# Two heads side by side in the TensorE array for the product of keys and values, with the last 64 tokens padded by zero rows

## The chip, the cores and the metric

The kernel runs on one core of a Trainium2 chip. The metric is the device time of one execution in microseconds (us), of which less is better. It is the median over several executions.

## The reference, cut to what matters

The program computes linear attention without a softmax, a norm of each head's output, and two feed-forward layers over all 8 x 576 = 4608 tokens. The part that the change touches is the first product, `kv`:

```python
# q, k, v: [batch 8, heads 8, tokens 576, 64] float32
kv  = np.einsum('bhsd,bhse->bhde', k, v)         # 64 x 64 for each head
out = np.einsum('bhsd,bhde->bhse', q, kv)
rms = np.sqrt(np.mean(out * out, axis=-1, keepdims=True) + 1e-06)
x   = out / rms * g_norm                          # then [4608, 512]
h = x @ w_in;  x = (h * sigmoid(1.702 * h)) @ w_out      # 512 -> 2048 -> 512
h = x @ w_in2; x = (s * relu(h) ** 2 + b) @ w_out2
```

## The kernel before, in words

The feed-forward layers take nearly all of TensorE's time. Each layer goes over nine blocks of 512 tokens, and each block over 16 chunks of d_ff. One such chunk of one block is a step. In a step `mm1` (lines 312 to 314) makes 12 passes of 512 columns for the first product of the layer, and `mm2` (lines 360 to 362 in the first layer, 364 to 366 in the second) makes 12 more for the second product, two steps later. Operands are split into a high and a low part, which is why there are three passes to each chunk.

Attention runs beside the steps, ahead of the block that needs it. For a batch `kv_pair(bb, p)` (lines 163 to 176) is called four times, once for two heads that lie next to each other. Its operands are tiles of 128 tokens x 128 columns, the 64 columns of one head and then the 64 of the other. So a product over the tokens gives 128 x 128 numbers, of which only the two 64 x 64 blocks on the diagonal are used. The 576 tokens are four chunks of 128 (line 169) and a rest of 64 (line 170), which reads a tile with 64 partitions. Such a product of float32 operands runs as two passes on TensorE, each with its own load of weights (LDWEIGHTS, PEld in the profile). A call is therefore ten passes, eight at line 169 and two at line 170.

`kv_out` (lines 178 to 185) copies the diagonal blocks of a batch from PSUM into `kvbd`, whose other blocks were set to zero by GpSimd at the start (line 491). `att_u` (lines 200 to 213) multiplies the queries of 128 tokens by `kvbd`. Where 128 tokens belong to two batches, 64 to each, it makes two products of 64 columns of weights, one into PSUM partitions 0 to 63 (line 212) and one into partitions 64 to 127 (line 213). There are four such token tiles (numbers 4, 13, 22 and 31).

The order of the work on each engine is the order of the program's text. The loop over steps in the last part of the function calls, in a step, `mm1`, then what the table `beside` holds under "pe" (here `kv_pair` and `att_u` are put by `kv_at` and `tile_at`), and then `mm2`. So in a step that has one, a `kv_pair` stands between line 314 and line 360. Batches 0 and 1 have their eight calls in the text ahead of the loop; batches 2 to 7 have theirs, 24 calls, in the loop. `load_rem` fetches the rests of the keys and values of a batch by SyncE's DMA queue (line 149), after the last `kv_pair` of the batch before has read the same buffer.

Of the kernel before, what the change touches and what calls it, by code (L numbers as in the profile page):

```python
# [8 lines left out]
F32 = mybir.dt.float32  # L9
# [6 lines left out]
P = 128  # L16
B, H, S, D = 8, 8, 576, 64
NT, DM, DFF = 4608, 512, 2048
NP = H // 2          # head pairs
KD = DM // P         # chunks of d_model  # L20
KF = DFF // P        # chunks of d_ff
BT = 512             # tokens of a block
NB = NT // BT
TT = BT // P         # token tiles of a block
#: While the first layer's weights become float32, two blocks share them: (block, from, to) in d_ff
#: chunks; what such a part leaves is added up when the second layer loads it.
CUTS = (0, 4, 8, 12, KF)
HEAD = [(j, lo, hi) for lo, hi in zip(CUTS, CUTS[1:]) for j in range(2)]
PARTS = HEAD + [(j, 0, KF) for j in range(2, 2 * NB)]
WARM = 8             # products that wake the tensor engine's clock  # L30
POOL = 8             # weights that GpSimd helps to split, while VectorE has the most to do
SM = 512             # tokens of a batch in whole chunks of 128
NC = SM // P
#: Of a float64's upper word, read as a float32: the exponent below float32's least, and where
#: float32 ends.
W_LEAST = 2.0 ** -15
# [4 lines left out]
def tile_attn_moe_moe2(  # L41
# [15 lines left out]
):  # L57
    """Float32 products in three passes of float32r: each operand is split exactly into
    H (12 significant bits, rounded) and L = x - H (the other 12)."""
    nc = tc.nc  # L60

    const = ctx.enter_context(tc.tile_pool(name="const", bufs=1))
# [3 lines left out]
    lp = ctx.enter_context(tc.tile_pool(name="lp", bufs=2))  # L66
# [10 lines left out]
    mhalf = const.tile([P, H], F32, name="mhalf")  # L77
    warm = const.tile([P, H], F32, name="warm")
    kvbd = [const.tile([P, NP, P], F32, name=f"kvbd{i}") for i in range(2)]

# [1 line left out]
    w_in, w_out = {}, {}  # L82
# [4 lines left out]
    def spare(name, shape):  # L87
        """A tile where weights come later."""
        return wp.tile(shape, F32, tag=name, name=f"s_{name}")
# [6 lines left out]
    def to_f32(which, ph, f):  # L96
        """float64 words to float32, rounded to nearest even: the exponent is rebased by bits,
        the 29 bits that go are rounded to one count of the last place that is added.
        A generator: other instructions go between its own."""
        raw = w_raw.pop((which, ph, f))  # L100
        lo, hi = raw[:, :, 0], raw[:, :, 1]
        w = lp.tile([P, DM], U32, tag="wf", name="wf", bufs=2)
        nc.scalar.activation(out=w.bitcast(F32), in_=hi.bitcast(F32), func=ACTF.Abs)
        nc.scalar.activation(out=lo, in_=lo, func=ACTF.Copy, scale=2.0 ** -29)
        yield
        # what float32 has no exponent for: 0 below it, the largest above it
        nc.vector.tensor_scalar(
            out=w.bitcast(F32), in0=w.bitcast(F32), scalar1=W_LEAST, scalar2=W_MOST, op0=ALU.max, op1=ALU.min
        )
        yield  # L110
        nc.vector.tensor_scalar(
            out=w, in0=w, scalar1=3, scalar2=0x3FFFFFF8, op0=ALU.logical_shift_left, op1=ALU.bitwise_and
        )
        yield
        nc.vector.scalar_tensor_tensor(
            out=w, in0=hi, scalar=0xC0000000, in1=w, op0=ALU.bitwise_and, op1=ALU.bitwise_or
        )
        yield
        nc.vector.tensor_tensor(out=w, in0=w, in1=lo, op=ALU.add)
        w_raw[which, ph, f] = w.bitcast(F32)  # L120
        yield
# [20 lines left out]

# [1 line left out]
    kt, vt, rem = {}, {}, {}  # L144

    def load_rem(bb):
        for nm, src in (("k", k_rest), ("v", v_rest)):
            t = lp.tile([P // 2, H * D], F32, tag=f"{nm}rem", name=f"{nm}rem", bufs=1)
            nc.sync.dma_start(out=t, in_=src[bb])
            rem[nm, bb] = t  # L150

# [11 lines left out]
    def kv_pair(bb, p):  # L163
        if bb not in kvps:
            kvps[bb] = ps_a.tile([P, NP, P], F32, tag="a", name="kvps")
        o = kvps[bb]
        kk, vv = kt.pop((bb, p)), vt.pop((bb, p))
        for c in range(NC):
            nc.tensor.matmul(o[:, p, :], kk[:, c, :], vv[:, c, :], start=(c == 0), stop=False)  # L169
        nc.tensor.matmul(  # L170
            o[:, p, :],
            rem["k", bb][:, p * P:(p + 1) * P],
            rem["v", bb][:, p * P:(p + 1) * P],
            start=False,
            stop=True,
        )

# [11 lines left out]
    def load_q(i, place=None):  # L189
        if place is None:  # L190
            q_t[i] = lp.tile([P, NP, P], F32, tag="q", name="qt", bufs=2)
        else:
            q_t[i] = spare(place, [P, NP, P])
        nc.sync.dma_start(out=q_t[i], in_=q[i].rearrange("p (a t) -> p a t", t=P))

    def early(i):
        # the first tiles use the PSUM of the feed-forward's sums, before there are any
        return dict(pool=ps_y, tag=f"y{i % TT}") if i < TT + 2 else dict(pool=ps_a, tag="a")

    def att_u(i):  # L200
        """Token-major q . kv of all heads."""
        qt = q_t.pop(i)
        e = early(i)
        u = u_t[i] = e["pool"].tile([P, H, D], F32, tag=e["tag"], name="u")
        b0, b1 = i * P // S, (i * P + P - 1) // S
        for p in range(NP):
            o = u[:, 2 * p:2 * p + 2, :]
            if b0 == b1:
                nc.tensor.matmul(o, qt[:, p, :], kvbd[b0 % 2][:, p, :], start=True, stop=True)  # L209
            else:  # L210
                m = b1 * S - i * P
                nc.tensor.matmul(o[0:m], qt[:, p, 0:m], kvbd[b0 % 2][:, p, :], start=True, stop=True)
                nc.tensor.matmul(o[m:P], qt[:, p, m:P], kvbd[b1 % 2][:, p, :], start=True, stop=True)
# [49 lines left out]

# [1 line left out]
    y_dram = {}  # L265
# [28 lines left out]

# [1 line left out]
    steps = [(j, f, lo, hi) for j, lo, hi in PARTS for f in range(lo, hi)]  # L296
    begin = {}                    # step at which a part begins
    for n, (j, f, lo, hi) in enumerate(steps):
# [84 lines left out]

# [1 line left out]
    beside = {}  # L385
# [8 lines left out]
    def tile_at(i, n, n_norm, n_turn, slot="turn"):  # L394
        """One tile of attention: what it is made of at step n, and when it is normed and turned."""
        at(n, "pe", att_u, i)
        at(n, "act", att_sq, i)
        at(n, "r", att_r, i)
        at(n_norm, "norm", att_norm, i)
        at(n_turn, slot, att_turn, i)  # L400
        early = "0" if slot == "pe" else ""
        at(n_turn, "xh" + early, att_xh, i)
        at(n_turn, "xl" + early, att_xl, i)

    def kv_at(bb, p, n):
        at(n, "pe", kv_pair, bb, p)
        if p + 2 < NP:
            at(n, "load", load_kv, bb, p + 2)
# [9 lines left out]

    # second block: most of it is begun before the steps
    at(5, "load", load_rem, 2)  # L420
# [9 lines left out]
    at(3, "xl0", att_xl, TT + 3)  # L430
    # third block
    n0 = begin[1, CUTS[-2]]
# [7 lines left out]
    tile_at(2 * TT + 3, n0 + 1, n0 + 2, n0 + 2)  # L440
    # the others
    for v_ in range(3, NB):
# [4 lines left out]
        for t in range(TT):  # L447
            n = n0 + 4 + 3 * t
# [9 lines left out]

    # weights: the first layer's in the order they are needed, then the second's through DRAM
    def need(w):  # L460
# [3 lines left out]

    order = sorted(((which, f) for f in range(KF) for which in (0, 1)), key=need)
    AHEAD = 3                     # before the first step
    convs = {}                    # by step
    first_w2 = 2 * KF + 2
    when = [(m - AHEAD, 0) + w for m, w in enumerate(order)]
# [12 lines left out]
    when = sorted([(n0 - 13 + f, 0, f) for f in range(KF)] + [(n0 - 5 + f, 1, f) for f in range(KF)])  # L482
# [5 lines left out]
    with tc.manual_schedule():  # L488
        make_identity(nc, ident)
        for t in kvbd:  # L490
            nc.gpsimd.memset(t, 0.0)
        nc.gpsimd.memset(mhalf, -0.5)
        # the activation table, and the tensor engine's clock, before there is work
        nc.scalar.activation(out=warm, in_=mhalf, func=ACTF.Sigmoid)
        o = ps_h.tile([P, BT], F32, tag="h", name="warm")
# [202 lines left out]
```

## Time and profile before

| | |
|---|---|
| median of three runs | 1697.47 us (1696.31 to 1697.64) |
| profiled execution: span, first to last instruction | 1694.9 us |
| of it, TensorE busy (PE) | 1677.7 us, 99% |
| weight loads busy (PEld) | 1391.6 us, 82% |
| VectorE / ScalarE / GpSimd busy | 716.4 / 574.6 / 72.4 us |
| passes on TensorE recorded | 7724 |

The profile is one execution. Its own time is known by its span only; the median of the runs is 2.6 us over that span, which takes in what lies ahead of the first instruction and behind the last. PE is the row of matmuls, PEld that of weight loads. A matmul's record lasts longer than the time until the next one starts, as matmuls are pipelined, so what a pass takes is read from the distance between starts.

### The profile page before, as it was taken

The page shows a single profiled execution, that of the slowest core. Times are in us where ns is not written, and L with a number is a line of the kernel's source. Part 1 is how long each engine was busy: PE and PEld are TensorE (multiplying, and loading weights), DVE is VectorE, ACT ScalarE, POOL GpSimd, SP SyncE. Part 2 cuts the span into 40 slices and gives each one's busy share as a digit, 9 for nine tenths or more (in the row PEclk, how much of TensorE's full clock was granted, in tenths as well). Part 3 has the DMA queues.
Part 4 walks back from the last instruction along what each step waited for, and adds up shares of the span by engine and source line. Part 5 has one row for each costly group of instructions (what it writes and reads, how often), then busy time and mean ns, then how long its engine had stood idle before and what let it go on. Part 6 is the DMA issues. An engine that isn't in the chain of part 4 may idle for free.

```text
span 1694.9 us, 19170 instructions
## 1 busy us (share of the span) xinstructions
PE 1677.7 (99%) x7724; PEld 1391.6 (82%) x7724; DVE 716.4 (42%) x1128; ACT 574.6 (34%) x957; POOL 72.4 (4%) x50
## 2 busy tenths in 40 slices
PE   8899999999999999999999999999999999999999
PEld 7688888888888888888888888888888888888887
DVE  5776634444353444444455533333233333333322
ACT  4566533333333333333334322222222222222222
POOL 3200100000000000001000000000000000000000
PEclk9999999999999999999999999999999999999999
DMA  6354523141313312121334210101010101000000
GB/s 224 118 174 153 178 95 92 56 123 58 131 53 103 94 57 91 59 75 57 112 107 144 92 50 1 50 1 50 1 50 1 50 1 38 12 20 31 1 25 25
DMA packets 57112, 120.78 MB, mean 71 GB/s; under 512 B 6848, under 2 KB 6848, under 8 KB 57024
## 3 DMA queue, kind: packets, MB, share of 16 engines
q1 hardware_dynamic: 57024, 119.57, 21.6%
q8 instruction: 60, 0.98, 0.3%
q14 instruction: 28, 0.23, 0.0%
HBM read 85.98 MB, written 33.55 MB: 71 GB/s over the span
## 4 chain that ended last, share of the span: by engine, by line
PE 97%; DVE 1%; DMA 1%; ACT 1%; issue 0%; SPq 0%; ACTq 0%; DVEq 0%
PE h L312 15%; PE h L313 15%; PE h L314 15%; PE acc L360 8%; PE acc L365 8%; PE acc L364 8%; PE acc L366 8%; PE acc L362 8%; PE acc L361 8%; PE kvps L169 2%; PE u L209 1%; PE xtp L238 1%; PE kvps L170 1%; DMA vt<-in_v 1%; DMA wraw<-in_w_out 0%
## 5 line engine op out<-in xcount | busy, mean ns | idle before, releaser
L312 PE MATMUL h<-xh,wih 128*128 128x512 f32 (+1 forms) x1156 | 452.0, 391 | 0.0
L314 PE MATMUL h<-xl,wih 128*128 128x512 f32 (+1 forms) x1156 | 449.1, 389 | 0.0
L313 PE MATMUL h<-xh,wil 128*128 128x512 f32 (+1 forms) x1156 | 449.1, 388 | 0.0
L314 PEld LDWEIGHTS h<-xl,wih 128*128 128x128 f32 x1156 | 217.0, 188 | 45.3
L312 PEld LDWEIGHTS h<-xh,wih 128*128 128x128 f32 x1156 | 217.2, 188 | 44.2
L313 PEld LDWEIGHTS h<-xh,wil 128*128 128x128 f32 x1156 | 217.1, 188 | 43.8
L325 DVE SCALAR_TENSOR_TENSOR g<-g,s_sb 128x512 f32<-128x512 f32 x144 | 108.3, 752 | 333.0 <-ACT g L324 333.0
L360 PE MATMUL acc<-gh,woh 128*128 128x512 f32 x576 | 230.9, 401 | 3.4 <-DVE xl L259 3.4
L324 ACT ACTIVATE g<-h 128x512 f32<-128x512 f32 x144 | 86.0, 597 | 430.4 <-PE h L314 430.4
L362 PE MATMUL acc<-gl,woh 128*128 128x512 f32 x576 | 225.6, 392 | 0.0
L361 PE MATMUL acc<-gh,wol 128*128 128x512 f32 x576 | 225.5, 391 | 0.1
L364 PE MATMUL acc<-woh,gh 128*128 128x512 f32 x576 | 224.1, 389 | 0.0
L365 PE MATMUL acc<-wol,gh 128*128 128x512 f32 x576 | 224.1, 389 | 0.0
L366 PE MATMUL acc<-woh,gl 128*128 128x512 f32 x576 | 224.1, 389 | 0.0
L321 ACT ACTIVATE g<-h 128x512 f32<-128x512 f32 x144 | 86.0, 597 | 348.7 <-PE h L314 348.6
L322 DVE TENSOR_TENSOR g<-g,h 128x512 f32<-128x512 f32 x144 | 98.9, 687 | 235.7 <-ACT g L321 235.4
L342 DVE SCALAR_TENSOR_TENSOR gl<-g,b_sb,gh 128x512 fp32r<-128x512 f32 x144 | 108.0, 750 | 175.4 <-PE acc L366 130.4
L334 ACT ACTIVATE gh<-g,b_sb 128x512 fp32r<-128x512 f32 x144 | 104.3, 724 | 118.7 <-DVE g L325 118.7
L340 DVE TENSOR_TENSOR gl<-g,gh 128x512 fp32r<-128x512 f32 x144 | 100.6, 699 | 96.7 <-PE acc L362 94.2
L360 PEld LDWEIGHTS acc<-gh,woh 128*128 128x128 f32 x576 | 108.7, 189 | 28.0 <-DVE xl L259 3.6
L362 PEld LDWEIGHTS acc<-gl,woh 128*128 128x128 f32 x576 | 108.7, 189 | 23.3
L332 ACT CAST gh<-g 128x512 fp32r<-128x512 f32 x144 | 89.5, 622 | 111.1 <-DVE g L322 111.1
(75 smaller groups left out, 1294.9 us busy)
## 6 DMA issues: line engine op xcount, KB each, us to landing
wraw<-in_w_in SPq DMA_DIRECT2D x32, 512.0 KB, 4.1
wraw<-in_w_out SPq DMA_DIRECT2D x32, 512.0 KB, 4.0
y<-ev SPq DMA_DIRECT2D x60, 256.0 KB, 2.2
yraw<-y SPq DMA_DIRECT2D x60, 256.0 KB, 3.9
out<-ev SPq DMA_DIRECT2D x36, 256.0 KB, 2.3
qt<-in_q SPq DMA_DIRECT2D x34, 256.0 KB, 4.5
w<-wf SPq DMA_DIRECT2D x32, 256.0 KB, 4.4
w2f<-w SPq DMA_DIRECT2D x32, 256.0 KB, 2.8
```

The costliest lines, as they stand in the source:

```text
L312: nc.tensor.matmul(o, wh[:, cs], xh[:, c, t0:t1], start=(c == 0), stop=False)
L313: nc.tensor.matmul(o, wl[:, cs], xh[:, c, t0:t1], start=False, stop=False)
L314: nc.tensor.matmul(o, wh[:, cs], xl[:, c, t0:t1], start=False, stop=(c == KD - 1))
L325: nc.vector.scalar_tensor_tensor(out=g, in0=g, scalar=s_sb[:, 0:1], in1=g, op0=ALU.mult, op1=ALU.mult)
L334: nc.scalar.activation(out=gh, in_=g_t[n], func=ACTF.Identity, bias=b_sb[:, 0:1])
L342: nc.vector.scalar_tensor_tensor(out=gl, in0=g, scalar=b_sb[:, 0:1], in1=gh, op0=ALU.add, op1=ALU.subtract)
L360: nc.tensor.matmul(o, wh[:, ds_], gh, start=first, stop=False)
L361: nc.tensor.matmul(o, wl[:, ds_], gh, start=False, stop=False)
L362: nc.tensor.matmul(o, wh[:, ds_], gl, start=False, stop=last)
L364: nc.tensor.matmul(o, gh[:, ds_], wh, start=first, stop=False)
L365: nc.tensor.matmul(o, gh[:, ds_], wl, start=False, stop=False)
L366: nc.tensor.matmul(o, gl[:, ds_], wh, start=False, stop=last)
```

## The change

`kv_pair` no longer multiplies two heads by two heads. For each chunk of tokens it makes two products of 64 columns of weights by 64 moving columns, one for each head. The first head's goes to PSUM partitions 0 to 63, the second's to partitions 64 to 127, and the two alternate. The rest of 64 tokens is read from tiles of 128 partitions, whose upper 64 partitions GpSimd sets to zero once at the start; the DMA goes on filling the lower 64. These tiles are allocated once and no longer taken from the pool `lp`, which held one buffer of each as well. Comments are taken out, which moves line numbers.

```diff
+    rem_t = {nm: const.tile([P, H * D], F32, name=f"{nm}rem") for nm in "kv"}
     kvbd = [const.tile([P, NP, P], F32, name=f"kvbd{i}") for i in range(2)]
...
     def load_rem(bb):
         for nm, src in (("k", k_rest), ("v", v_rest)):
-            t = lp.tile([P // 2, H * D], F32, tag=f"{nm}rem", name=f"{nm}rem", bufs=1)
-            nc.sync.dma_start(out=t, in_=src[bb])
-            rem[nm, bb] = t
+
+            nc.sync.dma_start(out=rem_t[nm][0:S - SM], in_=src[bb])
+            rem[nm, bb] = rem_t[nm]
...
         kk, vv = kt.pop((bb, p)), vt.pop((bb, p))
-        for c in range(NC):
-            nc.tensor.matmul(o[:, p, :], kk[:, c, :], vv[:, c, :], start=(c == 0), stop=False)
-        nc.tensor.matmul(
-            o[:, p, :],
-            rem["k", bb][:, p * P:(p + 1) * P],
-            rem["v", bb][:, p * P:(p + 1) * P],
-            start=False,
-            stop=True,
-        )
+
+        for c in range(NC + 1):
+            for h in range(2):
+                hs = slice(h * D, (h + 1) * D)
+                if c < NC:
+                    a, m = kk[:, c, hs], vv[:, c, hs]
+                else:
+                    w = slice(p * P + h * D, p * P + (h + 1) * D)
+                    a, m = rem["k", bb][:, w], rem["v", bb][:, w]
+                nc.tensor.matmul(o[hs, p, hs], a, m, start=(c == 0), stop=(c == NC))
...
         make_identity(nc, ident)
+        for t in rem_t.values():
+            nc.gpsimd.memset(t[S - SM:P], 0.0)
         for t in kvbd:
             nc.gpsimd.memset(t, 0.0)
         nc.gpsimd.memset(mhalf, -0.5)
```

TensorE's queue around the first `kv_pair` of batch 2 stood so before (output tile, operands, the output's partitions x columns, and how many products; each float32 product is two passes):

```order
L312 MATMUL h<-xh,wih_1115 128x512
L313 MATMUL h<-xh,wil_1116 128x512
L314 MATMUL h<-xl,wih_1115 128x512
L169 MATMUL kvps<-vt,kt 128x128 x4
L170 MATMUL kvps<-vrem,krem 128x128
L360 MATMUL acc_1341<-gh,woh_1405 128x512
L361 MATMUL acc_1341<-gh,wol_1406 128x512
```

And now, at a `kv_pair` of the same batch:

```order
L314 MATMUL h<-xh,wih_1202 128x512
L315 MATMUL h<-xh,wil_1203 128x512
L316 MATMUL h<-xl,wih_1202 128x512
L178 MATMUL kvps<-vt,kt 64x64 x8
L178 MATMUL kvps<-vrem,krem 64x64 x2
L362 MATMUL acc_1379<-gh,woh_1503 128x512
L363 MATMUL acc_1379<-gh,wol_1504 128x512
```

The place between the 12 passes of `mm1` and the 12 of `mm2` is the same; five products became ten of a quarter of the size.

GpSimd's queue at the start, before:

```order
masks.py:199 AFFINE_SELECT ident<-ident 128x128
L491 MEMSET kvbd_90 128x512
L491 MEMSET kvbd_91 128x512
L492 MEMSET mhalf 128x8
L227 TENSOR_TENSOR r<-ms,mhalf 128x8 x4
```

And now:

```order
masks.py:199 AFFINE_SELECT ident<-ident 128x128
L493 MEMSET krem 64x512
L493 MEMSET vrem 64x512
L495 MEMSET kvbd_92 128x512
L495 MEMSET kvbd_93 128x512
L496 MEMSET mhalf 128x8
L229 TENSOR_TENSOR r<-ms,mhalf 128x8 x4
```

Two memsets stand ahead of those of `kvbd` and `mhalf`. The queues of VectorE, ScalarE and SyncE (the DMAs) hold the same instructions in the same order as before.

## Rows read from the trace of the kernel before

**Rows 1.** The page, parts 1 and 2: busy time by engine, and TensorE's granted clock.

```profile
PE 1677.7 (99%) x7724; PEld 1391.6 (82%) x7724; DVE 716.4 (42%) x1128; ACT 574.6 (34%) x957; POOL 72.4 (4%) x50
...
PEclk9999999999999999999999999999999999999999
```

**Rows 2.** The page, part 4: the chain that ended last, by engine.

```profile
PE 97%; DVE 1%; DMA 1%; ACT 1%; issue 0%; SPq 0%; ACTq 0%; DVEq 0%
```

**Rows 3.** Windows: stretch, length, busy us (instructions) by engine, clock, DMA share, GB/s.

```profile
60.00:400.00 340.00, 339.94 (x1608) 282.05 (x1607) 185.33 (x319) 153.56 (x267) 23.34 (x13) 1.00 0.38 123
400.00:900.00 500.00, 500.00 (x2360) 415.24 (x2359) 227.05 (x374) 168.44 (x287) 29.35 (x17) 1.00 0.26 84
900.00:1694.00 794.00, 791.04 (x3490) 654.65 (x3489) 265.83 (x368) 224.99 (x356) 0.00 (x0) 1.00 0.10 33
```

**Rows 4.** Timeline of PE around one `kv_pair`: start us, length us, instructions merged.

```profile
639.74 0.39 PE L314 MATMUL h<-xl,wih 128*128 128x512 f32 x1
639.97 1.05 PE L169 MATMUL kvps<-vt,kt 128*128 128x128 f32 x8
640.95 0.48 PE L170 MATMUL kvps<-vrem,krem 64*128 64x128 f32 x2
641.37 0.50 PE L360 MATMUL acc<-gh,woh 128*128 128x512 f32 x1
641.70 0.40 PE L361 MATMUL acc<-gh,wol 128*128 128x512 f32 x1
```

**Rows 5.** Lines 169 and 170 from 60 us on: count, ns min/median/max, starts.

```profile
L169 PE MATMUL kvps<-vt,kt x192: 270/275/275, 153.1 to 647.7; 128*128 128x128 f32 x192
...
L170 PE MATMUL kvps<-vrem,krem x48: 272/322/373, 154.0 to 648.2; 64*128 64x128 f32 x48
```

**Rows 6.** Timeline of PE around the last token tile of two batches.

```profile
706.87 0.39 PE L314 MATMUL h<-xl,wih 128*128 128x512 f32 x1
707.19 0.32 PE L212 MATMUL u<-kvbd,qt 128*64 128x128 f32 x1
707.20 0.32 PE L213 MATMUL u<-kvbd,qt 128*64 128x128 f32 x1
707.35 0.27 PE L212 MATMUL u<-kvbd,qt 128*64 128x128 f32 x1
...
708.00 0.27 PE L212 MATMUL u<-kvbd,qt 128*64 128x128 f32 x1
...
708.21 0.50 PE L360 MATMUL acc<-gh,woh 128*128 128x512 f32 x1
708.55 0.40 PE L361 MATMUL acc<-gh,wol 128*128 128x512 f32 x1
```

**Rows 7.** Timeline of PEld (weight loads), the same place.

```profile
707.19 0.13 PEld L212 LDWEIGHTS u<-kvbd,qt 128*64 128x64 f32 x1 [0.35 <-issue]
...
707.24 0.14 PEld L212 LDWEIGHTS u<-kvbd,qt 128*64 128x64 f32 x1
```

**Rows 8.** The chain of the first 34 us in order of time: start us, us, what.

```profile
14.27 5.14 DMA vt<-in_v
...
30.32 0.03 ACT kvbd L181
```

**Rows 9.** Timelines of DVE and PE at 24 to 26 us.

```profile
24.17 0.68 DVE L231 TENSOR_TENSOR s_woh<-u,r 128x512 f32<-128x512 f32 x1
...
25.00 0.64 PE L238 MATMUL xtp<-ident,s_woh 128*128 128x128 f32 x4
```

**Rows 10.** Windows, columns as in rows 3: one at half clock, one at lines 212 and 213.

```profile
46.80:51.70 4.90, 4.88 (x12) 3.80 (x12) 4.14 (x7) 1.99 (x4) 2.29 (x2) 0.50 0.17 47
...
706.90:708.30 1.40, 1.40 (x19) 0.94 (x17) 0.31 (x1) 0.60 (x1) 0.00 (x0) 1.00 0.00 0
```

**Rows 11.** Timelines of POOL and ACT at the start.

```profile
1.25 0.98 POOL L491 MEMSET kvbd<- 128x512 f32 x2
...
12.50 0.36 ACT L181 COPY kvbd<-kvps 64x256 f32<-64x256 f32 x1 [9.97 <-PE kvps L170]
```

## The prediction

> **What bounds the kernel now.** I read the page first. TensorE is busy 99% of the span and its granted clock stands at the top digit in every slice [rows 1], and the chain of work that ended last is 97% TensorE [rows 2]. A busy PE alone proves little, because records of matmuls overlap, so the windows come next: from 60 us on PE is busy in all but 3 of 1634 us, at a clock of 1.00, while VectorE has 185 of 340 us at most [rows 3]. Nothing else holds TensorE up there. A pass that becomes shorter after 60 us therefore shortens the program by as much, and a saving on another engine is worth nothing. Before 60 us it is otherwise: the chain goes through a DMA and through ScalarE [rows 8].
>
> Next, what one `kv_pair` costs, from the timeline around one. The last ordinary pass before it starts at 639.74 and `kv_pair` at 639.97, so an ordinary pass of 512 columns takes 0.23. Line 361 starts at 641.70 [rows 4]. From 639.97 to 641.70 are 1.73 us; one ordinary pass (line 360) belongs in there, so the pair costs 1.73 - 0.23 = **1.50 us**. How much of it is streaming? Eight passes of line 169 last 1.05 together and a single one 0.27 [rows 4, 5], so they start (1.05 - 0.27)/7 = 0.111 apart. Ten at that pace would be 1.11. The other 0.39 lies around the two passes of line 170, which use 64 rows of the array: after 0.78 for seven starts the eighth is at 640.75, the next comes at 640.95 and not 0.11 later, line 360 comes late too, and line 361 stands 0.33 and not 0.23 behind it [rows 4]. Going over to another shape of the array and back costs 0.39 a pair.
>
> From 60 us on there are 192 + 48 passes of these two lines, which is 24 pairs [rows 5].
>
> **What the change puts there.** The trace already shows the new kind of work. Where a token tile belongs to two batches, lines 212 and 213 multiply by 64 columns of weights each, one into the lower and one into the upper half of the PSUM partitions, alternating. The two halves start 0.01 apart (707.19 and 707.20), and the next two only at 707.35 [rows 6]: the halves run side by side. I call such a couple of passes a slot. From the second start of line 212 at 707.35 to the eighth at 708.00 are six slots in 0.65, so 0.108 each [rows 6]. The whole tile, reckoned as above: from 706.87 to 708.55 are 1.68, less two ordinary passes of 0.23 gives 1.22; eight slots of 0.108 are 0.87; so getting into this shape and out of it costs 0.35. That is close to the 0.39 of today's change of shape. The new pair no longer has the 64-row passes (the rest is padded to 128 rows) but it does enter and leave the split shape, so I charge 0.35 and credit 0.39.
>
> The new pair has ten slots (five chunks of tokens, two passes each) of two halves. Here a slot's moving operand has 64 columns, while that of lines 212 and 213 has 128 [rows 6]. No row shows a slot of 64, so bounds. *From below:* if the time goes with the columns, half of 0.108 is 0.054; the weights for a slot cannot come faster than the first two loads of line 212 follow each other, 0.05 (707.19 and 707.24) [rows 7], and the loads keep the width of 64 that they have there. *From above:* 0.108, the same as with twice the columns. The weight loads say that at 128 columns it is the moving operand that sets the pace, as the next weights could be there in 0.05. So I take a value near the lower end, **0.06**, a little over it because moving operand and weights now need about the same time. The new pair is then 0.35 + 10 x 0.06 = 0.95, and the saving 1.50 - 0.95 = 0.55. Over 24 pairs that is **13.2 us**. At 0.054 it would be 0.61 a pair or 14.6; at 0.108 it is 0.07 a pair or 1.7.
>
> A rule speaks against the small passes. The sixteen passes of lines 212 and 213 start within 0.82 us, 0.051 us apart on average [rows 6]. The Trainium skill, "TensorE: Matmul & The Clock Gate", section "Wait — 56ns, not 53.3ns?", says that with hardware decode off each MATMUL takes about 62 ns in the sequencer, which binds when array work is shorter. By it a slot would take 0.124 as an estimate, and the 24 pairs would gain nothing. The trace does not agree: 0.051 is below 0.062.
>
> **The start (eight pairs, batches 0 and 1).** The pairs of batch 0 wait for their own DMAs, and those of batch 1 begin when a DMA lands at 14.27 + 5.14 = 19.4 [rows 8]. From there the chain runs through TensorE up to the copy at 30.3 [rows 8], so batch 1's four pairs count in principle. One is covered: the transposes behind the second pair start at 25.00, while VectorE gives their input at 24.17 + 0.68 = 24.85 [rows 9], so a faster second pair only waits there. Three pairs of 0.55 make 1.65; I take **1.5**, between 0 (the chain on VectorE and ScalarE takes it all up) and 8 x 0.61 = 4.9.
>
> **What costs nothing.** The two new memsets hold half as many partitions as those of `kvbd`, of which two take 0.98 [rows 11], so they delay `kvbd` and `mhalf` by 0.98 at most. The cover is the time until ScalarE copies into `kvbd` at 12.50 [rows 11]: `kvbd` is zero by 1.25 + 0.98 + 0.98 = 3.2. Without this cover it would be 0.98 once. The DMAs keep number, size, order and waits: they fill partitions that the memsets don't touch, and one buffer each is awaited as before. The copies of `kv_out` read the same blocks. Weight loads double in number but lie inside the slots.
>
> **Sum.** 13.2 + 1.5 = 14.7 us. From the span, 1694.9 - 14.7 = 1680.2; from the median, which is 2.6 above that span, 1697.47 - 14.7 = **1682.8**.
>
> **The rivals.**
> *The halves gain nothing from fewer columns.* A slot stays at 0.108, because something that doesn't shrink sets it: two weight loads of 0.05 in a row, say, or the load and then the pass. For it: no row has a slot of 64 columns. Against it: the second load of line 212 starts 0.05 after the first although line 213's load stands between them [rows 7], so the loads of the two halves also run side by side. Gain 1.7 and nothing at the start: 1695.8, which is within 0.2%. The same comes out if the halves are taken one after the other, that is, if the change doesn't do what it says. The skill has a rule for this one: "TensorE: Matmul & The Clock Gate", section "Part 3: Packing small matmuls — row/col tiling", says that weight loads overlap running matmuls only where they use other rows of the array, and here both halves use all rows. By it load and pass would add up. The trace doesn't agree: the second load of line 212 starts at 707.24, while the first slot's passes run until 707.35 [rows 6, 7], and the first slot, whose load nothing hides, takes 0.16, just 0.05 more than the later ones.
> *Entering and leaving is dearer with short slots.* If the change of shape costs 0.65 instead of 0.35, the pair saves 0.25: 24 x 0.25 = 6, with 0 to 1 at the start 1691. For it: the last pass before the exit is short and hides less. Against it: the 0.39 of today and the 0.35 of lines 212 and 213 agree at different lengths.
> *TensorE's clock falls.* With half as many columns in the array at a time, the granted clock could fall to its half level, 1.2 of 2.4 GHz, after each pair. From 46.8 to 51.7 it is at half, and twelve passes take 4.9 instead of 12 x 0.23 = 2.8, so such a stretch costs 2.1 [rows 10]. One after every pair would cost 24 x 2.1 = 50 against 13.2 gained: 1734, slower. It decides from seven such stretches on (13.2/2.1 = 6.3). Against it: at lines 212 and 213, with the same half-array loads for 1 us, the clock is at 1.00 [rows 10], and after 60 us it is 1.00 throughout [rows 3].
>
> **Chances and range.** Forecast 0.86; slots that gain nothing 0.08; dearer change of shape 0.03; the clock 0.03. A measurement can tell about 0.2% (3.4 us) from no change. Faster: 0.86 + 0.03 = 0.89; same: 0.08; slower: 0.03. The range of 8 in 10: at the fast end slots of 0.054 and some 4 at the start, 14.6 + 4 = 18.6, that is 1679; at the slow end slots of 0.07 and nothing at the start, 24 x 0.45 = 10.8, that is 1686.7, and 1.3 for what single runs differ by: 1688.
>
> **What would show it.** In the profile after, the lines of `kv_pair` should have no 64-row form, twice as many passes, and starts of one half 0.06 apart; the distance from its first start to the second pass of `mm2` should be 0.95 + 0.23 = 1.18 instead of 1.73 in all 24 places; PE stays at 99% and the clock at 1.00 after 60 us. I am wrong if the starts of one half are 0.1 apart, if the passes around the pair are late by more than 0.35 in sum, or if a stretch at half clock follows.

## The result, and the profile after

The changed kernel takes 1683.28 us (median of four runs, 1682.55 to 1684.06); the kernel before took 1697.56 (median of four runs, the three of the table above among them). The ratio is 0.9914, with a 95% interval of 0.9900 to 0.9928: faster by 0.86%. The forecast was 1682.8, in a range of 1679 to 1688.

The profiled execution has a span of 1680.8 us, 14.1 less than before. Busy time, clock and chain on its page, the lines that answer to [rows 1, 2]:

```profile
PE 1659.3 (99%) x8044; PEld 1371.7 (82%) x8044; DVE 715.5 (43%) x1128; ACT 573.7 (34%) x957; POOL 72.8 (4%) x52
...
PEclk9899999999999999999999999999999999999999
...
PE 96%; DVE 1%; DMA 1%; ACT 1%; issue 0%; SPq 0%; ACTq 0%; DVEq 0%
```

There are 320 passes more and TensorE is still busy for 99% of a shorter span. The clock has an 8 where it had only 9s; that slice belongs to the start, and more is said of it below. Around one `kv_pair` in the loop the timeline of PE now reads, against [rows 4]:

```profile
626.79 0.39 PE L316 MATMUL h<-xl,wih 128*128 128x512 f32 x1
627.10 0.69 PE L178 MATMUL kvps<-vt,kt 128*64 128x64 f32 x16
627.62 0.29 PE L178 MATMUL kvps<-vrem,krem 128*64 128x64 f32 x4
627.84 0.50 PE L362 MATMUL acc<-gh,woh 128*128 128x512 f32 x1
628.17 0.39 PE L363 MATMUL acc<-gh,wol 128*128 128x512 f32 x1
```

The 64-row form is gone and twenty passes stand where ten stood. From the last pass of `mm1` (626.79) to the second of `mm2` (628.17) are 1.38 us; with two ordinary passes of 0.23 taken off, the pair costs **0.92**. It was 1.50, and the forecast said 0.95.

Where does the span's 14.1 come from? The first pass of the same step's `mm1` in both traces, at the end of the start and behind the last `kv_pair`. Before:

```profile
150.34 0.39 PE L312 MATMUL h<-xh,wih 128*128 128x512 f32 x1
...
651.24 0.39 PE L312 MATMUL h<-xh,wih 128*128 128x512 f32 x1
```

And after:

```profile
150.41 0.39 PE L314 MATMUL h<-xh,wih 128*128 128x512 f32 x1
...
637.09 0.39 PE L314 MATMUL h<-xh,wih 128*128 128x512 f32 x1
```

At 150 us the changed kernel is 0.07 behind; at the end of the 24 pairs it is 14.15 ahead. So all of the gain comes from the loop, 14.2/24 = 0.59 a pair, and the start gave nothing in this execution. (0.59 is 0.01 to 0.02 more than 1.50 - 0.92: behind the pair, the rest of `mm2` takes 2.52 us instead of 2.54, from its second pass to the next step's first.)

### The profile page after: what moved, and what is told of

It is laid out like the page before. It is cut to its first block, busy times and chain, and to the rows that moved or that the text cites. A ratio compares the mean times of both kernels' runs of the same rounds, so it can differ in the third digit from the quotient of the medians.

```text
span 1680.8 us, 19812 instructions
## 1 busy us (share of the span) xinstructions
PE 1659.3 (99%) x8044; PEld 1371.7 (82%) x8044; DVE 715.5 (43%) x1128; ACT 573.7 (34%) x957; POOL 72.8 (4%) x52
## 4 chain that ended last, share of the span: by engine, by line
PE 96%; DVE 1%; DMA 1%; ACT 1%; issue 0%; SPq 0%; ACTq 0%; DVEq 0%
PE h L314 15%; PE h L316 15%; PE h L315 15%; PE acc L362 8%; PE acc L367 8%; PE acc L366 8%; PE acc L368 8%; PE acc L363 8%; PE acc L364 8%; PE u L211 1%; PE kvps L178 1%; PE xtp L240 1%; DMA vt<-in_v 1%; DMA s_woh<-in_q 0%; DMA wraw<-in_w_out 0%
```

## The experiments

The first four kernels ran on one chip and the last four on another, each group beside the kernel before. The medians of before were 1698.54 us in the first group (11 runs) and 1698.77 in the second (15 runs), so ratios are compared and not only times.

**Padding alone.** Both heads stay in one product; only the rest is read from 128 rows.

```diff
+    rem_t = {nm: const.tile([P, H * D], F32, name=f"{nm}rem") for nm in "kv"}
...
-            t = lp.tile([P // 2, H * D], F32, tag=f"{nm}rem", name=f"{nm}rem", bufs=1)
-            nc.sync.dma_start(out=t, in_=src[bb])
-            rem[nm, bb] = t
+            nc.sync.dma_start(out=rem_t[nm][0:S - SM], in_=src[bb])
+            rem[nm, bb] = rem_t[nm]
...
+        for t in rem_t.values():
+            nc.gpsimd.memset(t[S - SM:P], 0.0)
```

> The rest of 64 tokens is padded to 128 rows, but both heads stay in one product of 128 columns. Theory (the 64-row passes cost 0.39 us a pair by their change of shape, the rest is streaming): a pair becomes ten plain passes of 0.111, so 1.11 instead of 1.50; 24 x 0.39 = 9.4 us off, about 1688 us. Rival 1 (all of the gain comes from the two halves side by side, padding is worth nothing): as before, 1697. Rival 2 (all of the gain comes from padding): as the change, 1683.

Measured: 1687.98 us, ratio 0.9934 (0.9921 to 0.9948). The timeline of PE around a pair:

```profile
638.52 0.39 PE L314 MATMUL h<-xl,wih 128*128 128x512 f32 x1
638.75 1.05 PE L169 MATMUL kvps<-vt,kt 128*128 128x128 f32 x8
639.64 0.39 PE L170 MATMUL kvps<-vrem,krem 128*128 128x128 f32 x2
...
640.09 0.40 PE L361 MATMUL acc<-gh,wol 128*128 128x512 f32 x1
```

From 638.75 to 640.09 are 1.34, less one ordinary pass 1.11: ten plain passes of 0.111 and nothing else. The theory's number holds, both rivals fall. So about two thirds of the change's gain (0.39 of 0.58 a pair) is had without any splitting, by keeping the array in one shape. The split adds the smaller part, since it saves streaming but pays for a change of shape of its own.

**Halves alone.** The changed kernel, with the rest as 64 rows again.

```diff
-                    a, m = rem["k", bb][:, w], rem["v", bb][:, w]
+                    a, m = rem["k", bb][0:S - SM, w], rem["v", bb][0:S - SM, w]
```

> The two halves side by side, but the rest of 64 tokens read as 64 rows, without padding. Theory (each change of the array's shape makes the next passes wait for the last one and shows one load of weights): one more change within the pair, from 128 rows to 64 rows of the split shape, 0.09 for the wait and 0.05 for the load, so 0.15 more than the changed kernel: 24 x 0.15 = 3.6, about 1687 us. Rival 1 (rows don't count once the array is split): 1683. Rival 2 (the 64-row passes cost their whole 0.39 again): 1692.

Measured: 1685.76 us, ratio 0.9923 (0.9910 to 0.9935). The timeline of PE:

```profile
625.46 0.39 PE L316 MATMUL h<-xl,wih 128*128 128x512 f32 x1
625.77 0.69 PE L178 MATMUL kvps<-vt,kt 128*64 128x64 f32 x16
626.39 0.33 PE L178 MATMUL kvps<-vrem,krem 64*64 64x64 f32 x4
626.65 0.50 PE L362 MATMUL acc<-gh,woh 128*128 128x512 f32 x1
626.99 0.40 PE L363 MATMUL acc<-gh,wol 128*128 128x512 f32 x1
```

The passes of the rest start 0.62 behind the first ones and not 0.52, and the whole pair is 626.99 - 625.46 - 0.46 = 1.07, that is 0.15 more than in the changed kernel, as the theory had it. The time by itself lies between the theory's 1687 and rival 1's 1683; the pair's length in the trace decides for the theory, and so does the loop, which from 150 us on gains 10.8 in this profile against 14.2 for the change, 3.4 less. Rows count as a shape of their own even when the columns are split. Of the 0.15, 0.10 lies ahead of the rest and 0.04 behind its first passes (626.65 - 626.39 = 0.26 against 627.84 - 627.62 = 0.22), which fits the theory's wait and load.

**One head after the other.** The same products, in another order.

```diff
-        for c in range(NC + 1):
-            for h in range(2):
+        for h in range(2):
+            for c in range(NC + 1):
```

> The same 64x64 products as the changed kernel, but all ten passes of the first head ahead of all ten of the second, so that neighbours use the same half of the array. Theory (two halves run side by side only where neighbouring passes use different halves): 20 passes of 0.058 one after the other, 0.58 more a pair, 24 x 0.58 = 14, about 1697 us, the whole gain gone. Rival (short passes are cheap by themselves, whichever half they use): as the change, 1683.

Measured: 1694.45 us (seven runs), ratio 0.9970 (0.9959 to 0.9981). Most of the gain is gone, though the rest is still padded: without the halves running side by side the split shape costs more than it saves (1694.45 us against 1687.98 for padding alone), and short passes are not cheap by themselves. But the theory's 1697 was too much. The timeline of PE shows why:

```profile
624.59 0.73 PE L178 MATMUL kvps<-vt,kt 128*64 128x64 f32 x10
625.10 0.22 PE L178 MATMUL kvps<-vrem,krem 128*64 128x64 f32 x1
625.16 0.22 PE L178 MATMUL kvps<-vt,kt 128*64 128x64 f32 x1
625.16 0.22 PE L178 MATMUL kvps<-vrem,krem 128*64 128x64 f32 x1
625.22 0.46 PE L178 MATMUL kvps<-vt,kt 128*64 128x64 f32 x5
625.51 0.28 PE L178 MATMUL kvps<-vrem,krem 128*64 128x64 f32 x2
625.72 0.50 PE L362 MATMUL acc<-gh,woh 128*128 128x512 f32 x1
626.05 0.39 PE L363 MATMUL acc<-gh,wol 128*128 128x512 f32 x1
```

In the program's order the first head has eight passes from `vt` and then two from `vrem`, and only then comes the second head. Yet ten passes from `vt` start ahead of the first from `vrem`: at least two of the second head start before the first head's last two, and one more starts in between. So the passes of a free half start ahead of their turn, a few passes early. The pair costs 626.05 - 624.59 - 0.23 = 1.23 from its first start against 628.17 - 627.10 - 0.23 = 0.84, so 0.39 more and not 0.58. Three passes that run beside others save 3 x 0.058 = 0.17, nearly all of the difference.

**Two pairs in one step.** The pairs of batches 2 to 7 by twos, so the shape changes 12 times.

```diff
-        kv_at(2, p, n0 - 8 + p)
+        kv_at(2, p, n0 - 8 + (p | 1))
...
-                kv_at(v_, p, n0 + p)
+                kv_at(v_, p, n0 + (p | 1))
```

> The changed kernel with the pairs of batches 2 to 7 put in twos into one step (pairs 0 and 1 in the step of pair 1, pairs 2 and 3 in the step of pair 3), so that the array changes its shape 12 times and not 24. Theory (entering and leaving the split shape costs 0.35 each time): 12 x 0.35 = 4.2 us off the changed kernel, about 1679 us. Rival 1 (the change of shape is not what the 0.35 is, but a cost of each pair): 1683. Rival 2 (the second pair's keys and values come too late and TensorE waits): above 1683.

Measured: 1679.43 us, ratio 0.9885 (0.9871 to 0.9898). The timeline of PE:

```profile
617.03 0.69 PE L178 MATMUL kvps<-vt,kt 128*64 128x64 f32 x16
...
617.66 0.64 PE L178 MATMUL kvps<-vt,kt 128*64 128x64 f32 x16
618.13 0.29 PE L178 MATMUL kvps<-vrem,krem 128*64 128x64 f32 x4
618.34 0.50 PE L362 MATMUL acc<-gh,woh 128*128 128x512 f32 x1
618.68 0.39 PE L363 MATMUL acc<-gh,wol 128*128 128x512 f32 x1
```

The second pair follows without a gap. Its eight slots from 617.66 to 618.13 give the plainest reading of a slot, 0.47/8 = 0.059. Two pairs take 618.68 - 617.03 - 0.23 = 1.42 from the first start, against 2 x 0.84 = 1.68 apart. That is 0.26, and the wait of 0.09 ahead of the first start falls away once too: 0.35 saved for each change of shape that is left out, as forecast. Over the whole loop this profile goes from 1.15 behind the kernel before, at 150 us, to 17.62 ahead, so it gains 18.8 against the change's 14.2: 4.6 for twelve changes of shape, 0.38 each, of which about 0.02 is the longer `mm2` behind a pair. Rival 1 is out, and no wait for keys and values appears, so rival 2 is out too.

**The changed kernel again.**

> The changed kernel once more, beside the next three on the same chip: about 1683 us. Its trace shows whether the stretch at half clock at 57.7 to 61.2 us, which the kernel before did not have there, is there again (theory: such stretches belong to the waits of TensorE between 41 and 61 us and can lie differently from run to run).

Measured: 1682.37 us (1681.31 to 1683.51), ratio 0.9905 (0.9891 to 0.9918). Windows of this run and of the first one over the waits at the start (columns as in [rows 3]); first the changed kernel as profiled at first:

```profile
51.00:57.70 6.70, 3.43 (x16) 2.56 (x16) 6.48 (x11) 3.64 (x7) 1.29 (x1) 1.00 0.26 83
57.70:61.20 3.50, 2.85 (x9) 2.50 (x10) 2.11 (x4) 1.24 (x2) 0.00 (x0) 0.51 0.02 5
```

The same kernel again:

```profile
51.00:57.70 6.70, 3.43 (x16) 2.57 (x16) 6.48 (x11) 3.60 (x7) 1.29 (x1) 1.00 0.23 79
57.70:61.20 3.50, 2.81 (x15) 2.42 (x16) 2.49 (x4) 1.32 (x3) 0.00 (x0) 1.00 0.03 5
```

The work ahead of 57.7 is the same, and the granted clock from 57.7 to 61.2 is half in one execution and full in the other: 9 passes begun against 15. The stretch is not a property of the kernel. Its price is read from the next step's `mm1`. First the kernel before:

```profile
54.10 0.48 PE L312 MATMUL h<-xh,wih 128*128 128x512 f32 x1
...
62.91 0.39 PE L312 MATMUL h<-xh,wih 128*128 128x512 f32 x1
```

Then the changed kernel, first profile:

```profile
52.77 0.48 PE L314 MATMUL h<-xh,wih 128*128 128x512 f32 x1
...
62.87 0.39 PE L314 MATMUL h<-xh,wih 128*128 128x512 f32 x1
```

And again:

```profile
52.82 0.48 PE L314 MATMUL h<-xh,wih 128*128 128x512 f32 x1
...
61.61 0.39 PE L314 MATMUL h<-xh,wih 128*128 128x512 f32 x1
```

In both the change is 1.3 us ahead at 53 us. With the half clock all of it is lost by 62.9; without, 1.3 remains. It lasts: at 150 us, where the first profile stood at 150.41 and the kernel before at 150.34, the same pass is here at

```profile
149.17 0.39 PE L314 MATMUL h<-xh,wih 128*128 128x512 f32 x1
```

That is 1.2 ahead of the kernel before, and the span, 1679.5, is 15.4 shorter: 14.2 from the loop as in the first profile, and 1.2 from the start.

**Only the start changed.** Batches 0 and 1 with halves, batches 2 to 7 as before.

```diff
+        if bb >= 2:
+            for c in range(NC):
+                nc.tensor.matmul(o[:, p, :], kk[:, c, :], vv[:, c, :], start=(c == 0), stop=False)
...
+            return
```

> Only the eight pairs of batches 0 and 1 use the halves; batches 2 to 7 are as before, with 64 rows of the rest. Theory A (the prediction's term for the start): 1.5 us off, about 1696. Theory B (the trace after: 1.3 us ahead at 54 us, level with before at 63 us; the lead is lost to waits and to the clock): less than 0.7 us off, about 1697, and the passes of the third block's products start within 0.7 us of those of the kernel before.

Measured: 1697.75 us (11 runs), ratio 0.9997 (0.9988 to 1.0006): no difference that can be told. The time fits theory B better, though 0.9991 (theory A's 1.5 us) lies just inside the interval. Theory B's mark in the trace was missed by a little: level with before it is not, but 0.9 behind at 150 us. This execution had the half-clock stretch too (0.56 at 57.7 to 61.2).

**Passes that fill the waits.** Three times twelve extra passes, whose sums are overwritten by the real ones; only a PSUM tile is allocated earlier.

```diff
-        if t0 == 0:
+        if t0 == 0 and n not in h_t:
...
+    def fill(n, like):
...
         att_turn(TT + 1)
+        fill(2, 2)
...
+            if n == 3:
+                fill(4, 3)
             run(n, "pe")
...
+            if n == 2:
+                fill(3, 2)
             run(n, "turn")
```

> The changed kernel with 36 extra passes, whose sums are overwritten, in the three places between 41 and 61 us where TensorE waits for VectorE. Theory (the lead of the start is lost to stretches at half clock that follow these waits): the granted clock stays at 1.00 from 24 to 70 us, the products of the step that began at 62.9 begin 1.3 us earlier, and the time is about 1682. Rival (VectorE's chain of conversions ends last there, whatever the clock): that step begins at the same time, 1683 or more.

Measured: 1681.61 us (1681.29 to 1683.30), ratio 0.9902 (0.9889 to 0.9916). The window over the three waits:

```profile
42.00:62.00 20.00, 18.14 (x83) 14.30 (x84) 17.79 (x30) 10.19 (x18) 6.14 (x4) 1.00 0.24 79
```

The clock stays at 1.00 (in the profile of the next kernel, which has the same extra passes, too). From one step's `mm1` to the next the kernel needs as long as the runs without the half clock:

```profile
53.49 0.48 PE L314 MATMUL h<-xh,wih 128*128 128x512 f32 x1
...
62.31 0.39 PE L314 MATMUL h<-xh,wih 128*128 128x512 f32 x1
```

8.82 us, against 10.10 with the stretch and 8.79 without. The step begins 0.6 earlier than before and not 1.3, because this execution came into the stretch 0.7 later. In time it can't be told from the change itself (intervals 0.9889 to 0.9916 and 0.9891 to 0.9918).

**Twos and filled waits together.**

> The changed kernel with the pairs of batches 2 to 7 in twos and with the 36 extra passes. If both add up: 4.0 for the twos (as measured) and 1.3 for the clock, about 1678. If the extra passes gain nothing: 1679.4, as with the twos alone.

Measured: 1677.43 us, ratio 0.9874 (0.9859 to 0.9889), the fastest of all: 1.26% below before. Against the twos alone (0.9871 to 0.9898) the intervals overlap, so the part of the extra passes is not shown.

## Why the prediction was right, point by point

**The bound.** Passes that became shorter after 60 us shortened the program one for one: 14.15 us ahead at 637 us, 14.1 in the span.

**The pair's cost today (1.50, of it 0.39 for the 64-row passes).** Shown by padding alone, where exactly 0.39 goes.

**The new slot (0.06, bounds 0.054 and 0.108).** Measured 0.059 in the twos. Half the columns take 0.55 of the time (0.059 against 0.108), and it was right to stay near the lower end. The loads keep up: load and pass one after the other would have given about 0.11 in a slot (an estimate, 0.05 + 0.059), so the rival that a slot doesn't shrink is out. The Trainium skill, "TensorE: Matmul & The Clock Gate", section "Part 3: Packing small matmuls — row/col tiling", says that weight loads overlap running passes only where they use other rows, and also that a load into the background weight buffer can be pulled ahead of them. Here loads in the same rows overlap: slots of 0.059 leave no room for a load of 0.05 ahead of each pass. The prediction's 0.051 between starts is misread: sixteen starts within 0.82 have fifteen distances, of 0.055. The conclusion stands, and more clearly now: in the twos sixteen passes start in 0.47, 0.029 each, so 0.062 for each pass does not bind here.

**Getting in and out (0.35).** Measured 0.35 by leaving out half of the changes of shape. The rival of a dearer exit is out.

**The clock after the pairs.** From 60 us on it rounds to 1.00 in the windows of the profile after, two of which are shown, although the first still holds the end of a stretch at half clock that belongs to the start; from 61.2 to 400 us it is 1.00 as well. That rival is out.

```profile
60.00:400.00 340.00, 339.80 (x1757) 279.64 (x1756) 187.67 (x322) 154.83 (x272) 22.81 (x13) 1.00 0.37 123
...
900.00:1679.00 779.00, 776.89 (x3428) 643.18 (x3426) 258.07 (x357) 218.35 (x344) 0.00 (x0) 1.00 0.09 32
```

**The sum.** 13.2 + 1.5 = 14.7 was forecast. In the first profile 14.1 came, as 14.2 + 0, in the repeat 15.4, as 14.2 + 1.2. So the loop's term is shown and was 1.0 too low, and the start's 1.5 differs from one execution to the next; that the first sum came so close is in part luck, as its two terms were off in opposite directions. The loop's 24 pairs gave 0.59 each and not 0.55. The slot, taken a little too high, explains 0.01 to 0.02 of it, and the shorter rest of `mm2`, which the prediction did not count, about 0.02.

**The start.** This is the term that the runs do not settle. Its mechanism was half right. In the first profile batch 1 ends 1.3 earlier, and that by the pairs of batch 1: three of 0.55 less the 0.3 by which `vt` lands later are 1.35. Batch 0's gain is swallowed whole; the chain of the changed kernel at the start:

```profile
7.74 6.01 DMA s_woh<-in_q
...
13.77 5.95 DMA vt<-in_v
...
19.86 1.09 PE kvps L178 x20
...
29.01 0.03 ACT kvbd L183
```

Batch 0 is done 1.1 earlier (the copy by ScalarE starts at 11.42 instead of 12.50), but the next load of `vt`, which the chain now has behind the load of `q`, is issued only 0.5 earlier (13.77 instead of 14.27) and takes 5.95 instead of 5.14, so it lands 0.3 later than before. What the prediction left out is what comes after 30 us: TensorE waits three times for VectorE, 3.4, 1.4 and 2.6 us, and a stretch at half clock that begins at the end of the last of these waits takes the 1.3 back. Of the six profiles with halves at the start and no filled waits, five had such a stretch: the first of the change and the start alone at 57.7 to 61.2 us, the twos at 59.0 to 62.4, halves alone at 60.0 to 63.4 and one head after the other at 60.1 to 63.5. Only the repeat had none. The kernel before was profiled once, without it; how often it has one is not known. A further half microsecond goes at 147 us, where TensorE has to wait for a weight's low part:

```profile
147.19 0.39 PE L362 MATMUL acc<-gh,woh 128*128 128x512 f32 x1
147.78 0.50 PE L363 MATMUL acc<-gh,wol 128*128 128x512 f32 x1 [0.20 <-DVE wol L142]
```

The lead differs already ahead of these waits. In five profiles (the change, its repeat, the twos, and the two with filled waits) TensorE has the same 272 passes ahead of the first step with passes of 512 columns, and that step begins at 32.88, 32.92, 33.54, 33.56 and 35.09 us; in the kernel before it begins at 33.78. At 150 us the twos, with the same start as the change, are 1.2 behind the kernel before, where the repeat was 1.2 ahead:

```profile
151.50 0.39 PE L314 MATMUL h<-xh,wih 128*128 128x512 f32 x1
```

So one pair of profiles can't size this term, and the eleven runs of the start alone neither show 1.5 nor exclude it. The lower bound of the term, 0, was in the range, and so the range held.

**The memsets.** Forecast: 0.98 at most, and covered. They took more, and the cover held. GpSimd's timeline after:

```profile
1.36 0.52 POOL L493 MEMSET krem<- 64x512 f32 x1
...
2.40 0.99 POOL L495 MEMSET kvbd<- 128x512 f32 x2
```

`kvbd` is begun 1.15 later than in [rows 11] and is zero by 3.4, eight microseconds before it is needed.

## What to carry to other kernels

Before you split the array, look at what the present shape costs on its own: a tail with fewer rows cost 0.39 us each time here, and zero rows removed that without another change. A split pays by the streaming it saves less 0.35 for going in and out, so put the small products of one shape in one place; two pairs in a row were worth 4 us more. And don't count on a saving ahead of the first steady step: here the same passes were 1.2 us ahead of the kernel before in one execution and 1.2 behind in another by the time the loop's pairs began, and eleven runs showed no gain.

## What was not expected of the hardware

- With all passes of one half ahead of the other's, some of the second half's passes started before passes that stand ahead of them in the program: ten from `vt` where eight were due. The Trainium skill, "TensorE: Matmul & The Clock Gate", section "Part 3: Packing small matmuls — row/col tiling", says that matmuls start and end in program order. For passes in different column halves the starts in this trace don't agree.
- The same kernel on the same work had the granted clock at 0.51 in one execution and at 1.00 in another, in the same 3.5 us at the end of a wait and behind it, and this alone moved what followed by 1.3 us.
- A memset of 64 partitions x 512 took 0.52 us on GpSimd, as long as each of the two of 128 partitions x 512 (0.99 for both).
